# Four token tiles of the second layer, summed block by block beside w_out's conversion, in a one-core attention, cosine layer and expert-routing kernel

## The chip, the cores and the metric

The kernel runs on one core of a Trainium2 chip. The metric is the device time of one execution in microseconds; a lower number is better. The times below are medians of several runs; the rows come from one profiled execution, which has a time of its own.

## What is computed

Three stages follow each other; each takes the whole output of the one before.

```python
# 1. masked attention: 4 batches, 8 heads, 576 positions, head size 64
scores = scale * q @ k.T                  # heads 0-3: band of 32; heads 4-7: same position modulo 32
attn = softmax(where(masks, scores, -1e9)) @ v
x = attn.transpose(0, 2, 1, 3).reshape(2304, 512)
# 2. two layers with a cosine between them (d_ff = 2048)
h = x @ w_in
x = (h * cos(h)) @ w_out                  # 2304 x 512
# 3. routing to 8 experts with 288 places each, taken in order of all logits
logits = x @ w_gate
...
out[mask] = maximum(x[mask] @ w1[e], 0.0) @ w2[e]
```

Products are taken in float16 with a high and a low part, so that most matrix products are three matmuls: high by high, high by low, low by high. The input w_in and w_out are 8-byte floats and are converted on the chip.

## The kernel before, in words

A token tile is 128 of the 2304 tokens, so there are 18. A batch is 576 tokens. The **units** of the program are these; the short names are those used below.

- `att_pair(b, pr)` and `att_half(b, pr)` are a quarter of batch b's attention (two heads). They end in `x_parts`, which writes the layer's input x as two float16 parts into `xt`. VectorE takes row maxima, subtracts, sums and scales (tile `mxs` is in most of these).
- `load_w_in(f)` and `load_w_out(f)` fetch one of 16 blocks of a weight (512 KB) and convert it to two float16 parts. For w_out, VectorE, ScalarE and GpSimd share the work in `ar_t`; then a transposing DMA and eight small matmuls into PSUM bank `WP_BANK` = 7 multiply the block by w_gate (`wp`), so that later tiles can have their logits straight from layer one's output.
- `l1_unit(b, f)` is **layer one** for batch b and block f: two halves of 288 tokens, each 12 matmuls of 288 columns into one of PSUM banks 0 to 3; then a chain of ScalarE, VectorE and sometimes GpSimd gives h cos(h) as two float16 parts in `gt0` and `gt1` (tile `ar_g`). The bank is free when VectorE has read it the second time.
- `l2_tile(c)` is **layer two** for tile c: 48 matmuls of 512 columns over 16 blocks, three per block, into one bank; then ScalarE and VectorE write two parts into `ys`, which goes to DRAM. `early_logits(c)` transposes `ys` by DMA and takes the logits of tiles 0 to 4.
- `route` picks the experts (a long chain on VectorE with matmuls between), beside layer two of tiles 7 to 17. `experts` runs the eight experts.

The program first records tasks with what they read and write; `Plan.order` then sets the order on each engine. It keeps a clock of its own with an estimate for each task and takes, on each engine, the ready task with the highest priority: the length of the way to the end, plus a number by label from the table `BOOST`. The table `CHOICE` says for many small steps which engine does them. The order that comes out is fixed; on the chip, each engine runs its list from top to bottom and waits where it must. Until the first matmul of w_out's product the planner fills TensorE's planned gaps with **filler** matmuls of 128 columns that compute nothing (`p.filler`, line 609); the constant `fill_to` marks that first product, and after it there are none.

Before, layer one of batch 0 lay beside batch 1's attention; the conversion of w_out came after it, beside layer one of both batches; tiles 0 to 6 of layer two came after w_out, beside batch 2's attention:

```python
    for f in range(8):
        load_w_in(8 + f)
        l1_unit(0, 8 + f)
        l1_unit(1, f)
        if f % 2:
            load_w_out(f // 2)
```

The numbers of lines that the profile shows are those of helpers: 458 a matmul, 465 a transpose on TensorE, 482 and 485 ScalarE, 494 VectorE, 536 and 539 GpSimd, 543 a DMA, 547 a transposing DMA, 609 a filler.

Of the kernel before, what the change touches and what calls it, by code (L numbers as in the profile page):

```python
# [52 lines left out]
BOOST = {
    ('att', 0, 0, 0): 8538, ('att', 0, 0, 1): -17834, ('att', 0, 0, 2): 21893, ('att', 0, 0, 3): 254876, ('att', 0, 0, 4): -11936,
    ('att', 0, 1, 0): -88250, ('att', 0, 1, 1): 15713, ('att', 0, 1, 2): 6391904, ('att', 0, 1, 3): -16350,
    ('att', 0, 1, 4): 27537, ('att', 0, 2, 0): -15655, ('att', 0, 2, 1): -6151125, ('att', 0, 2, 2): 25706,
    ('att', 0, 2, 3): 18105, ('att', 0, 2, 4): -3603, ('att', 0, 3, 0): -102223, ('att', 0, 3, 1): 3933, ('att', 0, 3, 2): 4578,
    ('att', 0, 3, 3): 1293507, ('att', 0, 3, 4): 55587, ('att', 1, 0, 0): 385344, ('att', 1, 0, 1): -13827,
    ('att', 1, 0, 2): -3257, ('att', 1, 0, 3): 7190412552, ('att', 1, 0, 4): 30834, ('att', 1, 1, 0): 332375,
    ('att', 1, 1, 1): -28707, ('att', 1, 1, 2): 12945, ('att', 1, 1, 3): 293834, ('att', 1, 1, 4): -12205,  # L60
    ('att', 1, 2, 0): -14904, ('att', 1, 2, 1): -2120, ('att', 1, 2, 2): 19248, ('att', 1, 2, 3): 23623, ('att', 1, 2, 4): 9916,
    ('att', 1, 3, 0): -40947, ('att', 1, 3, 1): 410022, ('att', 1, 3, 2): 734082, ('att', 1, 3, 3): 205386,
    ('att', 1, 3, 4): -2577446, ('att', 2, 0, 0): 170034, ('att', 2, 0, 1): -130164, ('att', 2, 0, 2): 1120,
    ('att', 2, 0, 4): 13844, ('att', 2, 1, 0): 173621, ('att', 2, 1, 1): 176249, ('att', 2, 1, 2): -16793,
    ('att', 2, 1, 3): -27505, ('att', 2, 1, 4): -21043, ('att', 2, 2, 0): 227709, ('att', 2, 2, 1): 232256,
    ('att', 2, 2, 2): 21657, ('att', 2, 2, 3): 24684, ('att', 2, 2, 4): 12233196, ('att', 2, 3, 0): 245937,
    ('att', 2, 3, 1): -7701, ('att', 2, 3, 2): -3872, ('att', 2, 3, 3): 42822, ('att', 2, 3, 4): 4790463, ('att', 3, 0, 0): 20913,
    ('att', 3, 0, 1): -3804, ('att', 3, 0, 2): 27666, ('att', 3, 0, 3): -40439, ('att', 3, 0, 4): -70359, ('att', 3, 1, 0): -2201,
    ('att', 3, 1, 1): -10465, ('att', 3, 1, 2): -90149, ('att', 3, 1, 3): 936780, ('att', 3, 1, 4): -10007, ('att', 3, 2, 0): 2485,
    ('att', 3, 2, 1): -2493, ('att', 3, 2, 2): 16812, ('att', 3, 2, 3): -16129, ('att', 3, 2, 4): 18634, ('att', 3, 3, 0): 65330,  # L70
# [1629 lines left out]
```

## Time and profile before

| | |
|---|---|
| median of 3 runs | 774.19 us (773.64 to 775.09) |
| the profiled execution's own time | 779.23 us |
| its span in the trace | 777.4 us |
| TensorE busy | 716.3 us, 92% of the span |
| VectorE busy | 514.4 us, 66% |
| ScalarE busy | 424.6 us, 55% |
| GpSimd busy | 316.9 us, 41% |
| mean granted TensorE clock | 0.972 of full speed |

A share of the whole span is a mean over stages with different limits, so the rows below go by stretches. PE stands for TensorE, DVE for VectorE, ACT for ScalarE, POOL for GpSimd, SP for the queue that issues the DMAs. Times are in us from the span's start.

### The profile page before, as it was taken

The page shows a single profiled execution, that of the slowest core. Times are in us where ns is not written, and L with a number is a line of the kernel's source. Part 1 is how long each engine was busy: PE and PEld are TensorE (multiplying, and loading weights), DVE is VectorE, ACT ScalarE, POOL GpSimd, SP SyncE. Part 2 cuts the span into 40 slices and gives each one's busy share as a digit, 9 for nine tenths or more (in the row PEclk, how much of TensorE's full clock was granted, in tenths as well). Part 3 has the DMA queues.
Part 4 walks back from the last instruction along what each step waited for, and adds up shares of the span by engine and source line. Part 5 has one row for each costly group of instructions (what it writes and reads, how often), then busy time and mean ns, then how long its engine had stood idle before and what let it go on. Part 6 is the DMA issues. An engine that isn't in the chain of part 4 may idle for free. (4 is left out here: it accounts for less than half of the span.)

```text
span 777.4 us, 19249 instructions
## 1 busy us (share of the span) xinstructions
PE 716.3 (92%) x7714; PEld 515.1 (66%) x7714; DVE 514.4 (66%) x1392; ACT 424.6 (55%) x946; POOL 316.9 (41%) x344
## 2 busy tenths in 40 slices
PE   8999978999999999988999999997799989799986
PEld 7788756676455567666774555555687767577766
DVE  5787888989475777774568798878145435445550
ACT  3544967896444568986874243010146645555662
POOL 1538545486754025534431122011534446452531
PEclk9999989999999999999989999999799999899999
DMA  8944434566669644300023334001568879988771
GB/s 247 284 136 131 84 110 109 122 137 143 145 157 198 162 114 104 56 20 1 1 82 127 105 119 153 17 1 56 123 153 217 231 203 215 214 209 220 210 211 32
DMA packets 114265, 104.18 MB, mean 134 GB/s; under 512 B 79872, under 2 KB 89856, under 8 KB 114176
## 3 DMA queue, kind: packets, MB, share of 16 engines
q1 hardware_dynamic: 111104, 93.52, 47.8%
q0 software_dynamic: 3072, 9.44, 4.0%
q8 instruction: 60, 0.98, 0.5%
q14 instruction: 29, 0.24, 0.1%
HBM read 74.36 MB, written 9.70 MB: 108 GB/s over the span
## 5 line engine op out<-in xcount | busy, mean ns | idle before, releaser
L458 PEld LDWEIGHTS <-ar_l 128*128 128x128 f16 x2576 | 235.2, 100 | 98.9 <-issue 37.5
L458 PE MATMUL psum<-ar_w,ar_g 128*128 128x512 f16 (+2 forms) x1248 | 227.3, 319 | 2.8 <-DVE ar_w L494 1.8
L458 PE MATMUL psum<-ar_l 128*128 128x288 f16 (+2 forms) x1578 | 206.5, 286 | 20.8 <-DVE ar_l L494 17.8
L458 PEld LDWEIGHTS <-ar_g 128*128 128x128 f16 (+1 forms) x1944 | 151.4, 98 | 94.5 <-issue 7.0
L482 ACT ACTIVATE ar_l<-psum 128x288 int32<-128x288 f32 (+5 forms) x199 | 78.2, 424 | 73.3 <-PE psum L458 59.1
L494 DVE SCALAR_TENSOR_TENSOR ar_l<-ar_l,psum 128x288 f32<-128x288 int32 (+4 forms) x220 | 94.2, 449 | 36.1 <-ACT ar_l L482 35.1
L539 POOL TENSOR_TENSOR ar_l<-ar_l 128x288 f32<-128x288 f32 (+2 forms) x65 | 51.8, 800 | 157.1 <-DVE ar_l L494 82.0
L458 PEld LDWEIGHTS <-ar_t 128*128 128x128 f16 (+3 forms) x1900 | 73.0, 101 | 43.6 <-issue 11.8
L482 ACT ACTIVATE ar_g<-ar_l 128x512 f16<-128x512 f32 (+4 forms) x183 | 82.1, 474 | 35.3 <-DMA ar_l<-w 25.1
L539 POOL TENSOR_TENSOR ar_g<-ar_l,ar_g 128x288 f16<-128x288 f32 (+3 forms) x82 | 67.5, 830 | 57.4 <-ACT ar_g L482 56.7
L482 ACT ACTIVATE ar_l<-ar_l 128x512 f16<-128x512 f32 (+1 forms) x87 | 51.7, 623 | 53.5 <-DMA ar_l<-w 49.0
L482 ACT ACTIVATE ar_l<-ar_l,quarter 128x288 f32<-128x288 f32 (+1 forms) x124 | 64.6, 540 | 7.9 <-DVE ar_l L494 7.1
L458 PE MATMUL psum<-ar_g 128*128 128x288 f16 (+4 forms) x720 | 63.8, 264 | 5.1 <-ACT ar_g L482 2.5
L482 ACT ACTIVATE ar_t<-ar_t 128x512 uint32<-128x512 uint32 (+10 forms) x65 | 47.6, 747 | 37.5 <-DVE ar_t L494 8.7
L458 PE MATMUL psum<-ar_w,ar_t 128*128 128x512 f16 (+1 forms) x240 | 65.6, 336 | 0.0
L494 DVE SCALAR_TENSOR_TENSOR ar_l<-ar_l 128x512 f16<-128x512 f32 (+3 forms) x82 | 42.9, 546 | 31.8 <-ACT ar_l L482 29.3
L494 DVE SCALAR_TENSOR_TENSOR ar_t<-ar_t 128x512 uint32<-128x512 uint32 (+6 forms) x59 | 51.0, 867 | 14.6 <-ACT ar_t L482 14.6
L458 PE MATMUL psum<-ar_g,ar_l 128*128 128x96 f16 (+1 forms) x576 | 53.4, 255 | 7.5 <-DVE ar_w L494 4.4
L539 POOL TENSOR_TENSOR ar_t<-ar_t 128x512 uint32<-128x512 uint32 (+6 forms) x25 | 41.8, 1670 | 45.4 <-ACT ar_t L482 44.9
L458 PE MATMUL psum<-ar_w,ar_l 128*128 128x288 f16 x384 | 50.7, 295 | 3.7 <-DVE ar_w L494 3.7
L494 DVE SCALAR_TENSOR_TENSOR ar_g<-ar_l,ar_g 128x512 f16<-128x512 f32 x45 | 33.5, 768 | 29.7 <-ACT ar_g L482 28.9
L494 DVE SCALAR_TENSOR_TENSOR ar_w<-psum,ar_w 128x288 f16<-128x288 f32 x64 | 28.1, 451 | 27.1 <-ACT ar_w L482 26.5
(132 smaller groups left out, 829.4 us busy)
## 6 DMA issues: line engine op xcount, KB each, us to landing
...
```

The lines of the kernel that those rows point to most:

```text
L458: nc.tensor.matmul(o, l, x, start=start, stop=stop)
L482: p.add("act", ns, lambda: nc.scalar.activation(o, x, func, **kw), r, w, tab=tab)
L494: p.add("dve", 69.0 + 1.042 * n, lambda: getattr(nc.vector, name)(*args, **kw), r, w, ports=both)
L539: p.add("pool", 145.0 + (rate or (1.667 if y.dtype == F32 else 1.885)) * size(o), lambda: nc.gpsimd.tensor_tensor(o, x, y, op=op), r, w, p ...
```

## The change

Four tiles (0 to 3, `FIRST_TILES`) of layer two are recorded ahead of batch 1's layer one. All of w_in and of batch 0's layer one is recorded first, then w_out's 16 blocks with the rest of batch 1's attention between them, then the four tiles, then layer one of batch 1. Since the tiles 0 to 3 hold tokens of batch 0 alone, each needs only batch 0's layer one and those blocks of w_out that it has come to. Their outputs and transposed copies lie in that part of `gt1` that batch 1's layer one fills last (blocks 8 to 15), which is given a key of its own (`gB`), so that these writes wait until the four tiles are stored. The product of w_out and w_gate moves to columns 384 to 447 of bank 7 and the early logits to columns 480 to 495 of bank 4, with keys of their own (`wpb`, `lgp`) in place of the banks' keys. The tables `BOOST` and `CHOICE` are new nearly throughout: 373 of the 408 numbers of `BOOST` differ, 35 are gone and 17 new; of `CHOICE`, 24 entries differ, 84 are gone and 99 new.

```diff
-L2_GROUP, EARLY_TILES, EARLY_LOGITS, MORE_STAGE = 1, 7, 5, 8
+L2_GROUP, EARLY_TILES, EARLY_LOGITS, MORE_STAGE, FIRST_TILES = 1, 7, 5, 8, 4
...
-    ('att', 0, 0, 0): 8538, ('att', 0, 0, 1): -17834, ('att', 0, 0, 2): 21893, ('att', 0, 0, 3): 254876, ('att', 0, 0, 4): -11936,
...
-            mm(g, qk + kk_ + [("ident16",), ("mask16",)], pk(sbank[h]))
+            mm(g, qk + kk_ + [("ident16",), ("mask16",)], pk(sbank[h]) + ([("wpb",)] if sbank[h] == WP_BANK else []))
...
-        pw = bank[WP_BANK][:, :64].rearrange("p (f i e) -> p f i e", f=4, i=2)
+        pw = bank[WP_BANK][:, 384:448].rearrange("p (f i e) -> p f i e", f=4, i=2)
...
-        mm(g, [ck, ("wgh",)], pk(WP_BANK))
+        mm(g, [ck, ("wgh",)], [("wpb",)])
...
+    def gkey(key, f, i):
+
+        return (("gB" if key[0] == "gb" and f >= 8 else key[0]), *key[1:], f, i)
...
+        first = c < FIRST_TILES
...
+        yk = [("yt8", c)] if first else [("x", 1, pr, i, r) for pr in (2 * j, 2 * j + 1) for r in range(2)]
...
+        if first:
+            pl, bk = bank[4][:, 480:496], [("lgp",)]
+        else:
+            bi = take()
+            pl, bk = bank[bi][:, :16], pk(bi)
...
-    for f in range(8):
+    for f in range(16):
         load_w_in(f)
-        steps(att, 3 if f % 2 else 2)
         l1_unit(0, f)
-    steps(att, 2)
     p.reuse(["mask32", "stage1", "cv1"], ["woh", "wol"])
-    for f in range(8):
-        load_w_in(8 + f)
-        l1_unit(0, 8 + f)
+
+    yss[:] = [gt1[:, 1, 8 + 2 * c:10 + 2 * c].rearrange("p a b -> p (a b)") for c in range(FIRST_TILES)]
+    for f in range(16):
+        load_w_out(f)
+        steps(att, 1 + f % 2)
+    for c in range(FIRST_TILES):
+        yi, ys = l2_tile(c, hbank)
+        early_logits(c, ys, yi, hbank)
+    steps(att, 100)
+    p.reuse(["ys", "yt8"], ["gB"])
+    for f in range(16):
         l1_unit(1, f)
-        if f % 2:
-            load_w_out(f // 2)
-    for f in range(8):
-        load_w_out(4 + f)
-        l1_unit(1, 8 + f)
-    for f in range(12, 16):
-        load_w_out(f)
...
-    for c in range(early_tiles):
+    steps(att, 5 * FIRST_TILES)
+    for c in range(FIRST_TILES, early_tiles):
         yi, ys = l2_tile(c, hbank)
```

Three places show what this does to the lists of the engines. The first is the start of the DMA queue's list. In the rows `kl`, `q` are the inputs of batch 0's first attention quarter, `w_in` a block of 512 KB. Before:

```order
L543 DMA ar_w<-mask 128x304
L543 DMA ar_g<-kl 128x352
L543 DMA ar_g<-q 128x320
L543 DMA ar_g<-kl 128x256
L543 DMA ar_g<-q 128x256
```

And of the change:

```order
L570 DMA ar_t<-w_in 128x4x256 x2
L570 DMA ar_w<-w_in 128x4x256 x2
L570 DMA ar_w<-mask 128x304
L570 DMA ar_w<-w_in 128x4x256
L570 DMA wg<-w_gate 128x32
L570 DMA ar_g<-kl 128x352
L570 DMA ar_g<-q 128x320
L570 DMA ar_g<-kl 128x256
```

Five blocks of w_in now stand ahead of the first attention input. On TensorE, 711 fillers stand in the list of the change where 507 stood: 234 ahead of the first attention matmul (35 before), and 516 ahead of the first matmul of layer one (128 before). The other 6870 matmuls are the same in number.

The second place is TensorE's list right behind the product of w_out's block 6 with w_gate (`wgh`). A row `ar_l 128x288` is a matmul of layer one, `ar_w,ar_g 128x512` one of layer two. Before:

```order
L458 LDWEIGHTS ar_t
L458 MATMUL psum<-wgh,ar_t 128x8
L458 LDWEIGHTS ar_l
L458 MATMUL psum<-ar_l 128x288
L458 LDWEIGHTS ar_l
L458 MATMUL psum<-ar_l 128x288
```

And of the change:

```order
L485 LDWEIGHTS ar_t
L485 MATMUL psum<-wgh,ar_t 128x8
L485 LDWEIGHTS ar_g
L485 MATMUL psum<-ar_w,ar_g 128x512
L485 LDWEIGHTS ar_g
L485 MATMUL psum<-ar_w,ar_g 128x512
L485 LDWEIGHTS ar_l
L485 MATMUL psum<-ar_l 128x288
```

The first matmuls of tile 0 stand there, with nine blocks of w_out to come; between this block and the last one the list holds 126 matmuls of layer two, where 74 stood before.

The third place is VectorE's list in batch 2's attention (`mxs`), around its second block of scores. `ar_l<-ar_l,psum 128x288` is a step of a layer-one unit. Before:

```order
L494 TENSOR_REDUCE mxs<-psum 128x5
L494 TENSOR_REDUCE mxs<-psum 128x4
L494 TENSOR_TENSOR ar_t<-psum,mxs 128x480
L494 TENSOR_TENSOR ar_t<-psum,mxs 128x384
L494 TENSOR_REDUCE mxs<-ar_t 128x5
L494 TENSOR_SCALAR lgl_78<-psum 128x8
L494 SCALAR_TENSOR_TENSOR ar_t<-ar_t 128x1152
L494 SCALAR_TENSOR_TENSOR lg<-psum,lgl_78 128x8
L494 TENSOR_REDUCE mxs<-ar_t 128x4
```

And of the change:

```order
L521 SCALAR_TENSOR_TENSOR ar_l<-ar_l,psum 128x288
L521 TENSOR_REDUCE mxs<-psum 128x5
L521 TENSOR_REDUCE mxs<-psum 128x4
L521 TENSOR_TENSOR ar_t<-psum,mxs 128x480
L521 TENSOR_TENSOR ar_t<-psum,mxs 128x384
L521 TENSOR_SCALAR lgl_77<-psum 128x8
L521 SCALAR_TENSOR_TENSOR ar_l<-ar_l,psum 128x288
L521 SCALAR_TENSOR_TENSOR lg<-psum,lgl_77 128x8
L521 TENSOR_REDUCE mxs<-ar_t 128x5
L521 TENSOR_REDUCE mxs<-ar_t 128x4
```

Batch 2's attention now shares VectorE with layer one of batch 1; before it stood between evictions of layer-two tiles.

## Rows read from the trace of the kernel before

**Rows 1.** The page: its head, and what the DMAs moved in 40 slices.

```profile
span 777.4 us, 19249 instructions
...
GB/s 247 284 136 131 84 110 109 122 137 143 145 157 198 162 114 104 56 20 1 1 82 127 105 119 153 17 1 56 123 153 217 231 203 215 214 209 220 210 211 32
```

**Rows 2.** Busy time of each engine in seven stretches of the span.

```profile
core 0: us, PE busy (x) PEld busy (x) DVE busy (x) ACT busy (x) POOL busy (x), PEclk, DMA share, GB/s
0.00:90.70 90.70, 85.52 (x1339) 71.66 (x1340) 69.84 (x152) 47.70 (x113) 43.37 (x51) 1.00 0.66 186
90.70:178.00 87.30, 76.46 (x689) 58.35 (x687) 77.92 (x162) 70.49 (x186) 52.68 (x60) 0.96 0.49 115
178.00:272.00 94.00, 92.94 (x946) 51.34 (x945) 62.81 (x115) 46.02 (x89) 42.64 (x34) 1.00 0.72 161
272.00:346.00 74.00, 67.99 (x931) 51.45 (x928) 55.89 (x126) 62.73 (x132) 32.35 (x28) 1.00 0.35 77
346.00:398.00 52.00, 48.34 (x407) 37.86 (x406) 28.05 (x61) 39.93 (x105) 23.05 (x30) 1.00 0.05 16
398.00:546.00 148.00, 140.62 (x1436) 79.86 (x1434) 121.11 (x600) 40.31 (x72) 25.16 (x39) 0.96 0.24 81
546.00:777.40 231.40, 204.43 (x1980) 164.60 (x1980) 98.81 (x183) 117.41 (x253) 97.60 (x105) 0.94 0.76 188
```

**Rows 3.** PE's waits: in 90.7:178, in 272:346, and two in 346:398.

```profile
PE psum L458 <- DVE ar_l L494: 10.8, 12, 4.3
...
PE psum L458 <- DVE ar_l L494: 5.7, 8, 1.3
...
PE psum L458 <- ACT ar_l L482: 2.6, 3, 1.3
PE psum L458 <- DVE ar_l L494: 1.0, 2, 0.6
```

**Rows 4.** The filler's tile; then busy time of line 609 in two stretches.

```profile
L609 PE MATMUL psum<-quarter x507: 216/222/314, 0.9 to 90.6; 128*128 128x128 f16 x169
...
0.00:4.40 4.40, 3.51 (x34) 3.51 (x35) 1.00 0.53 149
38.50:41.40 2.90, 2.72 (x47) 2.73 (x48) 1.00 0.61 187
```

**Rows 5.** Groups by form: layer one 346.5:396, layer two 247.5:256, VectorE 132:207, 207:272.

```profile
L458 PE MATMUL psum<-ar_l 128*128 128x288 f16 x364 | 46.1, 286 | 3.7 <-ACT ar_l L482 2.6 <-DVE ar_l L494 1.0
...
L458 PE MATMUL psum<-ar_w,ar_g 128*128 128x512 f16 x34 | 7.5, 379 | 0.0
...
L494 DVE SCALAR_TENSOR_TENSOR ar_l<-ar_l,psum 128x288 f32<-128x288 int32 x35 | 15.3, 448 | 3.7 <-ACT ar_l L482 3.5
L494 DVE TENSOR_SCALAR ar_t<-ar_t 128x512 uint32<-128x512 uint32 x11 | 7.4, 673 | 1.9 <-PE psum L458 1.3 <-POOL ar_w L539 0.6
...
L494 DVE SCALAR_TENSOR_TENSOR ar_t<-psum,ar_t 128x512 f16<-128x512 f32 x5 | 3.4, 686 | 0.7 <-ACT ar_t L482 0.7
```

**Rows 6.** Busy time of each engine in two stretches, columns as in Rows 2.

```profile
132.00:207.00 75.00, 70.75 (x580) 49.34 (x579) 63.87 (x127) 56.56 (x152) 54.31 (x58) 1.00 0.57 128
...
207.00:272.00 65.00, 64.15 (x735) 34.34 (x734) 41.50 (x75) 28.87 (x44) 20.93 (x13) 1.00 0.78 175
```

**Rows 7.** The same of instructions on tile ar_t alone, in three stretches.

```profile
34.00:97.00 63.00, 17.88 (x374) 13.72 (x374) 26.09 (x42) 13.17 (x31) 20.75 (x18) 1.00 0.47 132
...
132.00:207.00 75.00, 4.16 (x96) 4.02 (x96) 26.85 (x35) 11.75 (x19) 27.53 (x22) 1.00 0.57 128
...
207.00:272.00 65.00, 12.07 (x405) 10.40 (x405) 29.83 (x40) 25.29 (x35) 20.93 (x13) 1.00 0.78 175
```

**Rows 8.** Instructions on tile mxs, 34:104: busy DVE, ACT, POOL, then clock.

```profile
34.00:104.00 70.00, 13.68 (x32) 2.30 (x9) 6.84 (x4) 1.00 0.45 127
```

**Rows 9.** Busy time in the stretch at the lower granted clock, columns as in Rows 2.

```profile
108.40:115.30 6.90, 4.48 (x19) 2.75 (x19) 6.54 (x15) 5.57 (x14) 4.65 (x5) 0.51 0.47 153
```

**Rows 10.** PE's longest wait in 546:777.4: us in total, times, longest.

```profile
PE psum L458 <- DVE ar_w L494: 10.6, 7, 3.9
```

More of the change, by code (lines that the diff above doesn't have):

```diff
@@ L50 @@
 S_BANKS, S2_BANKS, X_BANKS, T_BANKS, WP_BANK = (4, 4), (4, 7), (5, 6), (7,), 7
-L2_GROUP, EARLY_TILES, EARLY_LOGITS, MORE_STAGE = 1, 7, 5, 8
+L2_GROUP, EARLY_TILES, EARLY_LOGITS, MORE_STAGE, FIRST_TILES = 1, 7, 5, 8, 4
 BOOST = {
-    ('att', 0, 0, 0): 8538, ('att', 0, 0, 1): -17834, ('att', 0, 0, 2): 21893, ('att', 0, 0, 3): 254876, ('att', 0, 0, 4): -11936,
[L55 to L70, printed above, removed]
[72 rows of a table removed]
@@ new lines @@
+    ('att', 0, 0, 0): 64768, ('att', 0, 0, 1): 180, ('att', 0, 0, 2): 123215, ('att', 0, 0, 3): 372907, ('att', 0, 0, 4): -61505,
+    ('att', 0, 1, 0): -30903, ('att', 0, 1, 1): 3914, ('att', 0, 1, 3): -29192, ('att', 0, 1, 4): 1103431, ('att', 0, 2, 0): 40980,
+    ('att', 0, 2, 1): 1914, ('att', 0, 2, 2): 1937, ('att', 0, 2, 3): -196979022, ('att', 0, 3, 0): 9004, ('att', 0, 3, 1): -1977,
+    ('att', 0, 3, 2): 1888421, ('att', 0, 3, 3): 40429, ('att', 0, 3, 4): 64601, ('att', 1, 0, 0): 532, ('att', 1, 0, 1): 21303,
@@ new lines @@
+    ('att', 1, 1, 0): 554072, ('att', 1, 1, 1): -486, ('att', 1, 1, 3): 644979, ('att', 1, 1, 4): -1647, ('att', 1, 2, 0): 215,
+    ('att', 1, 2, 1): -288897, ('att', 1, 2, 2): 61280369, ('att', 1, 2, 3): 211675996, ('att', 1, 2, 4): -44884,
+    ('att', 1, 3, 0): 66239546, ('att', 1, 3, 1): 1912602, ('att', 1, 3, 2): -16835267,
+    ('att', 1, 3, 3): 2292248208926377539181100400640, ('att', 1, 3, 4): 32451, ('att', 2, 0, 0): 40171891,
+    ('att', 2, 0, 1): 60380, ('att', 2, 0, 2): -396115, ('att', 2, 0, 3): 11289, ('att', 2, 0, 4): 4621, ('att', 2, 1, 0): 653038,
@@ new lines @@
+    ('att', 2, 1, 1): 390, ('att', 2, 1, 2): -16698, ('att', 2, 1, 3): 207087, ('att', 2, 1, 4): -25471, ('att', 2, 2, 0): 138573,
+    ('att', 2, 2, 1): 141862, ('att', 2, 2, 2): 11323, ('att', 2, 2, 3): 4966, ('att', 2, 2, 4): 281999176557,
+    ('att', 2, 3, 0): -1126, ('att', 2, 3, 1): -364522544032689451672166440056582256332202049536, ('att', 2, 3, 3): -6305,
+    ('att', 2, 3, 4): -43370778662819572853743805874402027687116800,
+    ('att', 3, 0, 0): 101041401800544194786443176735291514269204480, ('att', 3, 0, 2): -43294, ('att', 3, 0, 3): -73,
@@ L143 @@
+    ('att', 3, 0, 4): 9222, ('att', 3, 1, 2): -10643, ('att', 3, 1, 3): 4688129, ('att', 3, 1, 4): -5518516531986,
+    ('att', 3, 2, 0): -115, ('att', 3, 2, 1): -314, ('att', 3, 2, 2): 16713, ('att', 3, 2, 3): -8722721700,
+    ('att', 3, 2, 4): -17524, ('att', 3, 3, 0): 668, ('att', 3, 3, 1): 487558, ('att', 3, 3, 2): -108061,
[93 rows of a table added]
 }
 CHOICE = {
-    ('cvi', 0): 'pool', ('cvi', 2): 'pool', ('cvi', 9): 'pool2', ('cvi', 10): 'pool', ('cvi', 14): 'pool', ('cvo', 5): 'pool2',
+    ('cvi', 0): 'psum', ('cvi', 2): 'pool', ('cvi', 9): 'pool2', ('cvi', 10): 'pool', ('cvi', 14): 'pool', ('cvo', 5): 'pool2',
@@ L197 @@
-    ('pts', 0, 0, 2): 'dve', ('pts', 0, 1, 2): 'dve', ('pts', 0, 2, 0): 'dve', ('pts', 0, 2, 1): 'dve', ('pts', 0, 2, 2): 'dve',
-    ('pts', 0, 3, 0): 'dve', ('pts', 0, 3, 1): 'dve', ('pts', 0, 3, 2): 'dve', ('pts', 1, 0, 0): 'dve', ('pts', 1, 0, 1): 'dve',
-    ('pts', 1, 0, 2): 'dve', ('pts', 1, 1, 0): 'dve', ('pts', 1, 2, 2): 'dve', ('pts', 1, 3, 1): 'dve', ('u', 0, 0): 'halves',
[14 rows of a table removed]
-    ('ylo', 8): 'dve', ('ylo', 9): 'dve', ('ylo', 11): 'dve', ('ylo', 12): 'dve', ('ylo', 13): 'dve', ('ylo', 15): 'dve',
@@ L215 @@
-    ('yt', 0, 1): 'act', ('yt', 2, 0): 'dve',
+    ('ewa', 0, 'w1', 0, 512): 'pool2', ('ewa', 0, 'w1', 1, 0): 'pool', ('ewa', 0, 'w1', 1, 512): 'pool',
+    ('ewa', 0, 'w1', 2, 0): 'pool', ('ewa', 0, 'w1', 3, 512): 'pool', ('ewa', 0, 'w2', 3, 0): 'pool',
+    ('ewa', 0, 'w2', 7, 0): 'pool', ('ewa', 1, 'w1', 1, 0): 'pool2', ('ewa', 1, 'w1', 1, 512): 'pool',
+    ('ewa', 1, 'w1', 2, 0): 'pool', ('ewa', 1, 'w1', 3, 512): 'pool', ('ewa', 1, 'w2', 5, 0): 'pool',
+    ('ewa', 2, 'w1', 0, 0): 'pool', ('ewa', 2, 'w1', 1, 512): 'pool', ('ewa', 2, 'w1', 3, 0): 'pool',
[4 rows of a table added]
@@ new lines @@
+    ('ewa', 4, 'w2', 5, 0): 'pool', ('ewa', 4, 'w2', 6, 0): 'pool2', ('ewa', 5, 'w1', 1, 0): 'pool',
+    ('ewa', 5, 'w1', 2, 0): 'pool2', ('ewa', 5, 'w1', 3, 0): 'pool2', ('ewa', 5, 'w2', 0, 0): 'pool',
+    ('ewa', 5, 'w2', 7, 0): 'pool2', ('ewa', 6, 'w1', 0, 0): 'pool', ('ewa', 6, 'w1', 0, 512): 'pool2',
+    ('ewa', 6, 'w1', 1, 0): 'pool', ('ewa', 6, 'w1', 2, 512): 'pool', ('ewa', 6, 'w2', 1, 0): 'pool2',
+    ('ewa', 6, 'w2', 2, 0): 'pool', ('ewa', 6, 'w2', 3, 0): 'pool2', ('ewa', 6, 'w2', 4, 0): 'pool',
@@ new lines @@
+    ('ewa', 7, 'w1', 1, 0): 'pool', ('ewa', 7, 'w1', 1, 512): 'pool2', ('ewa', 7, 'w1', 2, 512): 'pool',
+    ('ewa', 7, 'w2', 6, 0): 'pool', ('exp', 0, 0): 'bias', ('exp', 0, 1): 'bias', ('exp', 1, 1): 'bias', ('g', 0, 4, 1): 'pool',
[24 rows of a table added]
+    ('hv', 2, 0): 'pool', ('hv', 3, 1): 'pool', ('hv', 3, 3): 'pool', ('mul', 0, 1): 'dve', ('mul', 0, 2): 'dve',
+    ('mul', 2, 1): 'pool', ('mul', 2, 3): 'pool', ('mul', 3, 0): 'pool', ('mul', 3, 2): 'pool', ('og', 0, 0, 0): 'act',
[12 rows of a table added]
+    ('oh', 6, 3, 1): 'dve', ('plo', 2, 1): 'pool', ('plo', 2, 2): 'pool', ('plo', 2, 3): 'pool', ('plo', 3, 0): 'pool',
@@ new lines @@
+    ('plo', 3, 3): 'pool', ('pts', 0, 3, 1): 'dve', ('pts', 1, 0, 0): 'dve', ('pts', 1, 0, 1): 'dve', ('pts', 1, 0, 2): 'dve',
+    ('pts', 1, 1, 0): 'dve', ('pts', 1, 2, 2): 'dve', ('u', 0, 0): 'halves', ('u', 0, 1): 'halves', ('u', 0, 2): 'halves',
[14 rows of a table added]
+    ('xl', 0, 3, 0): 'pool', ('xl', 1, 2, 0): 'pool', ('xl', 1, 3, 0): 'pool', ('ylo', 8): 'dve', ('ylo', 9): 'dve',
+    ('ylo', 11): 'dve', ('ylo', 12): 'dve', ('ylo', 13): 'dve', ('ylo', 15): 'dve', ('yt', 0, 0): 'dve', ('yt', 0, 1): 'act',
+    ('yt', 2, 0): 'dve', ('yt', 2, 1): 'act',
@@ L477, in act_fixed @@
     def act_fixed(r):
-        return 51.0 if any(k[0] == "ps" for k in r) else 92.0
+        return 51.0 if any(k[0] in ("ps", "wpb", "lgp") for k in r) else 92.0
     def act(o, x, func, r, w, tab=None, **kw):
@@ L491, in call @@
             def call(n, r, w, *args, **kw):
-                on_psum = any(k[0] == "ps" for k in list(r) + list(w))
+                on_psum = any(k[0] in ("ps", "wpb", "lgp") for k in list(r) + list(w))
                 both = not on_psum and name in ("tensor_tensor", "scalar_tensor_tensor", "tensor_scalar", "tensor_copy")
@@ L972, in load_w_out_ @@
             lk = [("lgl", li)]
-            act(ll, pw[:, :, 1], AF.Copy, pk(WP_BANK), lk, scale=1.0 / WOUT_SCALE)
-            dve.scalar_tensor_tensor(32, pk(WP_BANK) + lk, lk, ll, pw[:, :, 0], 1.0 / WOUT_SCALE, ll, op0=ALU.mult, op1=ALU.add)
+            act(ll, pw[:, :, 1], AF.Copy, [("wpb",)], lk, scale=1.0 / WOUT_SCALE)
+            dve.scalar_tensor_tensor(32, [("wpb",)] + lk, lk, ll, pw[:, :, 0], 1.0 / WOUT_SCALE, ll, op0=ALU.mult, op1=ALU.add)
             act(wp[:, fs, :NE], ll, AF.Copy, lk, k0)
@@ L1040, in l1_unit_ @@
             for lo, hi, gt, at, keys in pieces:
-                k0, k1 = ([(*k, f, i) for k in keys] for i in range(2))
+                k0, k1 = ([gkey(k, f, i) for k in keys] for i in range(2))
                 gh, gl = (gt[:, i, f, at:at + hi - lo] for i in range(2))
@@ L1065, in g_segments @@
                     segs.append([gt, at + lo, hi - lo, keys])
-        return [(gt, o, n, lambda f, keys=keys: [(*k, f, i) for k in keys for i in range(2)]) for gt, o, n, keys in segs]
+        return [(gt, o, n, lambda f, keys=keys: [gkey(k, f, i) for k in keys for i in range(2)]) for gt, o, n, keys in segs]
     def logits(c0, take, after=()):
@@ L1096, in early_logits @@
         i, j = divmod(c % 4, 2)
-        yt = xt[1][:, i, 2 * j:2 * j + 2, :].rearrange("p k t -> p (k t)")[:, :1024].rearrange("p (i k t) -> p i k t", i=2, t=128)
-        yk = [("x", 1, pr, i, r) for pr in (2 * j, 2 * j + 1) for r in range(2)]
+        first = c < FIRST_TILES
+        yt = gt1[:, 0, 8 + 2 * c:10 + 2 * c].rearrange("p a b -> p (a b)").rearrange("p (i k t) -> p i k t", i=2, t=128) if first else xt[1][:, i, 2 * j:2 * j + 2, :].rearrange("p k t -> p (k t)")[:, :1024].rearrange("p (i k t) -> p i k t", i=2, t=128)
+        yk = [("yt8", c)] if first else [("x", 1, pr, i, r) for pr in (2 * j, 2 * j + 1) for r in range(2)]
         dma_t(yt.rearrange("p i k t -> p (i k) t"), ys, [("ys", yi, j, h) for j in range(2) for h in range(2)], yk)
-        bi = take()
-        pl = bank[bi][:, :16]
+        if first:
[3 more added lines that the diff above has]
+            pl, bk = bank[bi][:, :16], pk(bi)
         g = []
@@ L1105, in early_logits @@
             g.append((pl[:, :NE], yt[:, 1, k], wgh[:, 0, k, :], False, k == 3))
-        mm(g, yk + [("wgh",)], pk(bi))
+        mm(g, yk + [("wgh",)], bk)
         ll, lk = rot("lgl", lgl)[::-1]
         scale = 1.0 / (WOUT_SCALE * Y_SCALE)
-        dve.tensor_scalar(8, pk(bi), [("lgl", lk)], ll[:, 0], pl[:, NE:], scale, None, op0=ALU.mult)
-        dve.scalar_tensor_tensor(8, pk(bi) + [("lgl", lk)], [("lg", c // 3 * 3)], lg[:, c, :], pl[:, :NE], scale, ll[:, 0],
+        dve.tensor_scalar(8, bk, [("lgl", lk)], ll[:, 0], pl[:, NE:], scale, None, op0=ALU.mult)
+        dve.scalar_tensor_tensor(8, bk + [("lgl", lk)], [("lg", c // 3 * 3)], lg[:, c, :], pl[:, :NE], scale, ll[:, 0],
                                  op0=ALU.mult, op1=ALU.add)
@@ L1519 @@
     p.label = None
-    p.reuse(["pqt", "pkt", "pvt", "psb", "ppts", "pxf"], ["ga", "gb", "gc"])
+    p.reuse(["pqt", "pkt", "pvt", "psb", "ppts", "pxf"], ["ga", "gb", "gc", "ys", "yt8"])
     ar_g.at = 0
@@ L1610 @@
         p.series = None
-    p.reuse(["gb"], ["w11", "w21"])
+    p.reuse(["gb", "gB"], ["w11", "w21"])
     p.reuse(["ga", "gc"], ["yt", "yg", "og", "ot"])
```

14 lines of the change are left out of this document (removed), and 268 rows, old and new, of tables (BOOST, CHOICE).

## The prediction

> **What bounds the kernel now.** I read the busy time by stretch first [rows 2]. TensorE is the busiest engine in every stretch but one, so the question for each stretch is how long TensorE stood still and for whom. Up to 90.7 it shows 85.5 busy of 90.7, but the fillers' tile [rows 4] says that 507 of the matmuls there compute nothing; the last one starts at 90.6. In this part VectorE (69.8 busy) and the arriving weights set the pace and TensorE is padded. From 90.7 to the end of layer one at 398, TensorE is busy for 76.5 + 92.9 + 68.0 + 48.3 = 285.7 of 307.3, so 21.6 are lost. The chain of waits names the loser's partner [rows 3]: 10.8 for VectorE in 90.7:178, where w_out is converted beside layer one and VectorE is busy for 77.9 of 87.3; 5.7 for VectorE in 272:346, where batch 3's attention lies beside layer one of batch 2; 2.6 for ScalarE and 1.0 for VectorE in 346:398. In 178:272, where layer two gives TensorE long work that asks little of VectorE, only 1.1 are lost. From 398 on (routing beside layer two, then the experts) the change edits no code but tables.
>
> So the kernel is bound by TensorE where layer two is at hand and by VectorE where conversions, attention and layer one meet. The change moves layer two to the first kind of trouble, and leaves the second kind, batch 2's attention, without part of it.
>
> **The change, term by term.**
>
> *More fillers.* 711 − 507 = 204 fillers are added, and TensorE runs its list in order, so each is paid. In mid-program 47 fillers take 2.72 [rows 4], 0.058 each; 204 × 0.058 = **+11.8**. They don't come on top of real work done in the same time: they stand where real work stood. At the last filler the list of before has 520 real matmuls behind it and that of the change 399, of which 36 missing ones are layer one's (46.1 / 364 = 0.127 each [rows 5], 4.6) and 85 batch 1's attention (17.9 / 374 = 0.048 per record and two records for many [rows 7], so 4 to 8). That makes 9 to 12, about what the fillers take; so the last filler ends at about the same time as before, near 91, with some 12 of work still to do. Is VectorE further by then, so that this is paid back? By its list, the work ahead of that point is w_in nearly whole instead of two thirds, but less of the attention and of layer one: 132 instructions against 147. I take no gain.
>
> *The start.* The first scores now stand behind five blocks of w_in and the mask, some 3.1 MB. At the first slice's 247 GB/s [rows 1] that is 12.6. The 234 fillers ahead of them take 35 at 3.51 / 34 = 0.103 [rows 4] and 199 at 0.058, in all 15.1, from 0.9 on: until 16.0. The load is hidden by 3.4; should it take longer than that, the rest would be paid in full, since every later attention step follows it. Taken as nothing.
>
> *Stretch I, from the last filler to w_out's last block.* TensorE's list: 288 matmuls of layer one (36.5), 126 of layer two at 7.5 / 34 = 0.22 [rows 5] (27.8), and 241 small ones at 0.043 to 0.048 [rows 7] (11): 75. VectorE's: twelve units of layer one, fourteen blocks of w_out, half of batch 1's attention. Prices from 132:207, where nothing else runs on it: 63.9 busy [rows 6], of which 26.9 on `ar_t` [rows 7] and about 2.5 for the product with w_gate are w_out's, and 34.5 layer one's. The 35 first steps are 17.5 units, the 11 conversions 11 blocks [rows 5]; so 2.0 per unit and 2.7 per block. 24 + 37 + half of 13.7 [rows 8] = 68, or 0.90 of TensorE's.
>
> *Stretch II, from there to the end of layer one of batch 1.* TensorE: 384 of layer one (48.8), 98 of layer two (21.6), 378 small ones at 12.07 / 405 = 0.030 [rows 7] (11): 81.5. VectorE: 16 units (32), four evictions at 0.69 [rows 5] (2.8), and batch 2's attention with its loads: 41.5 busy in 207:272 [rows 6] less 3.4 for five evictions and 1.6 for logits = 36.5. Together 71, or 0.87. Before, this attention had layer two beside it.
>
> *Stretch III, to the end of layer one of batch 2*, holds what 272:346 held, with 112 matmuls of layer two (24.7) in place of 27: TensorE 68.0 + 85 × 0.22 = 87, VectorE about 60 (55.9 and the end of batch 2's attention), 0.69. *Stretch IV* is batch 3's layer one as before.
>
> *What is lost in them.* The trace gives loss against load: at a ratio of VectorE to TensorE of 0.68 (178:272) 1% of TensorE's time, at 0.82 (272:346) 9%, at 1.02 (90.7:178) 14% [rows 2]. Between these, 0.90 gives 11% of 75 = 8.3, and 0.87 gives 10% of 81.5 = 8.2. Layer two in the list can run while VectorE catches up, so I take off its share of TensorE's work (27.8 of 75, 21.6 of 81.5): 5.2 and 6.0. For III I take 2.5 (between 1.3, by the ratio, and the 6.0 of 272:346), for IV the 3.7 of now. In all **17.4** where 21.6 are lost now. Bounds: below, nothing in I and II, 6.2 in all; above, 14% in both, 6.0 and 3.7, in all 32.
>
> *The clock.* In 108.4:115.3 the granted clock is 0.51, the lower of the two levels, 1.2 GHz; the longest wait of rows 3, 4.3, lies just ahead of it. TensorE was busy for 4.48 of these 6.9 [rows 9]; at 2.4 GHz it would need half, so up to 2.2 come back if the wait goes and the clock stays up. I take **−1.1**. The Trainium skill ("TensorE: Matmul & The Clock Gate", section "Terms") puts the penalty at the throttled time times what is missing of the clock, here 3.4; the row gives less, since a third of that stretch had no matmul to slow. With the page's figure taken whole, the sum below would be 4.2 instead of 6.5.
>
> *At nothing:* the keys `wpb` and `lgp` only take waits away, and PE's waits show none for that product; tiles 0 to 3 are stored and transposed once as before, only sooner. The new wait is that of `gB`: batch 1's layer one may not write block 8 until the fourth tile's logits are read. Behind it would stand ScalarE and VectorE, and TensorE for their banks. But 98 matmuls stand on TensorE between those logits and block 8's first half, 60 of them layer one's (7.6); a store and a transpose have that long. Were the cover gone, it would cost what is missing of a few microseconds once. From 398 on: the same matmuls, other tables. TensorE loses 27 of the last 231.4 there [rows 2], 10.6 of them in its longest wait [rows 10]; I take 0 and bounds of ±3, about a tenth of it.
>
> *The sum.* 11.8 − 21.6 + 17.4 − 1.1 = **+6.5**. On the span 777.4 this makes 783.9, and with the 1.8 that the profiled execution has around its span, 785.7. That execution, 779.23, stands 5.0 above the median of the runs, 774.19; so I forecast a median of **780.7**.
>
> **The rivals.** *Faster.* Layer two's blocks, three matmuls each, cover all of VectorE's lag in I and II, and the losses fall to 6.2; with the clock kept, 11.8 − 21.6 + 6.2 − 2.2 = −5.8, **768.4**. It decides at losses of 9.4: below, the change wins by more than 0.2% (1.55 of 774.19, about what a measurement tells from no change). For it speaks 178:272, where 1% is lost beside layer two; against it, that VectorE had 0.68 there and has 0.87 to 0.90 now, and that layer two is a third and a quarter of the list instead of two thirds.
>
> *No change.* Losses of 9.4 to 12.5, a little under what the ratio and the cover give: **774**.
>
> *Much slower.* The small share of layer two covers nothing, since a bank must be free for its tile too, and both stretches lose 14%: 11.8 − 21.6 + 32 = +22, **796**. Against it: VectorE's ratio is lower than where 14% was lost.
>
> That the change does not do what it says is excluded: the lists show layer two between w_out's blocks.
>
> **How the numbers follow.** My forecast, slower by 1.6 to 14: 0.54. Much slower, beyond that: 0.10. Faster: 0.23. No change: 0.13. So slower 0.64. The forecast's own range is 776 to 788. For 8 in 10, I leave one tenth at each end: **769 to 790**, from nearly all of the faster case to past the forecast's end.
>
> **What would show it.** After: the last filler near 91 and 711 of them, not 507, the last busy time of line 609; PE's wait for VectorE in the w_out stretch 4 to 7 instead of 10.8; a new wait for VectorE of 4 to 8 where `mxs` and `ar_l` steps alternate, at 170 to 260; layer one of batch 3 ending near 404 to 405 instead of 398; from there to the end 379 as now. The step most likely to fail is the loss in I and II: if PE waits less than 3 in either, the forecast is too high. If the last filler comes well before 88, the first term is wrong, and if it comes after 94, the start is.

## The result and the profile after

The change makes the kernel slower: 785.75 us (median of 4 runs, 784.71 to 786.54) against 774.50 of the kernel before (4 runs, 773.64 to 775.09), a ratio of 1.0145, 95% interval 1.0128 to 1.0163. That is +11.25, where +6.5 was forecast (780.7; 785.75 lies in the range 769 to 790). A second set of runs gave 783.99 against 774.20, 1.0114 (1.0081 to 1.0147), +9.8. So the sign and the range held, and the size was 3 to 5 too small. The profiled execution of the change has an own time of 784.71 and a span of 782.6.

Busy time of each engine in seven stretches of the change, cut at the last filler, w_out's last block, the end of layer one of batches 1, 2 and 3, the end of routing and the end of TensorE's work (columns as in [rows 2], which cut the kernel before at other times; ends of parts, here and below, are those of the last matmul of the part in TensorE's list):

```profile
0.00:89.30 89.30, 85.46 (x1357) 74.67 (x1358) 72.30 (x139) 47.00 (x108) 37.99 (x43) 1.00 0.71 216
89.30:171.70 82.40, 77.61 (x748) 50.63 (x746) 66.39 (x133) 59.04 (x136) 48.98 (x46) 0.98 0.52 129
171.70:259.90 88.20, 81.67 (x865) 56.81 (x863) 67.05 (x151) 72.26 (x153) 29.29 (x33) 1.00 0.50 126
259.90:350.10 90.20, 85.30 (x1056) 59.70 (x1054) 60.00 (x130) 67.11 (x142) 35.43 (x33) 1.00 0.30 76
350.10:401.30 51.20, 49.99 (x492) 39.91 (x490) 30.32 (x67) 41.69 (x110) 23.55 (x31) 1.00 0.02 6
401.30:551.20 149.90, 138.75 (x1436) 79.37 (x1434) 121.46 (x592) 41.68 (x75) 30.69 (x45) 0.97 0.24 84
551.20:775.60 224.40, 203.28 (x1982) 162.65 (x1981) 96.65 (x166) 118.97 (x257) 115.15 (x126) 0.95 0.77 193
```

Length minus TensorE's busy time, the first two numbers behind each stretch, is what TensorE lost: 3.8 up to the last filler, then 4.8, 6.5, 4.9 and 1.2 up to the end of layer one, together 17.4. The forecast for stretches I to IV was 17.4. Layer one ends at 401.3 (397.9 before). Up to there the change loses 3.4. Unless the shown profile of before is itself too long up to there (the second profile below answers this), the rest of the 11 lies behind it, where only the tables differ.

The filler's tile in the change, which answers to [rows 4]:

```profile
L636 PE MATMUL psum<-quarter x711: 216/222/315, 0.9 to 89.2; 128*128 128x128 f16 x178
```

PE's waits in 89.3:171.7, in 171.7:259.9 and in 259.9:350.1, which answer to [rows 3] (what is waited for: us in total, times, longest):

```profile
PE psum L485 <- DVE ar_l L521: 1.4, 4, 0.7
PE psum L485 <- ACT ar_l L509: 1.3, 1, 1.3
PE psum L485 <- DMA ar_t<-ar_w: 1.1, 2, 0.8
...
PE psum L485 <- DVE ar_l L521: 4.7, 6, 1.5
...
PE psum L485 <- DVE ar_l L521: 2.8, 4, 1.1
```

Beside w_out's conversion the wait for VectorE fell from 10.8 to 1.4; a new one of 4.7 stands beside batch 2's attention. PE's waits from the end of routing on, which answer to [rows 10]:

```profile
PE psum L485 <- ACT ar_g L509: 10.3, 5, 4.3
PE psum L485 <- DVE ar_w L521: 6.3, 7, 2.0
PE psum L485 <- DMA ar_g<-y_dram,idx: 3.8, 1, 3.8
```

The wait for ScalarE on `ar_g` is new in this size: in the experts ScalarE writes there the high parts of every second expert's weights.

### The profile page after: what moved, and what is told of

It is laid out like the page before. It is cut to its first block, busy times and chain, and to the rows that moved or that the text cites. A ratio compares the mean times of both kernels' runs of the same rounds, so it can differ in the third digit from the quotient of the medians.

```text
span 782.6 us, 19708 instructions
## 1 busy us (share of the span) xinstructions
PE 722.2 (92%) x7918; PEld 523.7 (67%) x7918; DVE 514.2 (66%) x1374; ACT 448.3 (57%) x979; POOL 322.0 (41%) x357
## 4 chain that ended last, share of the span: by engine, by line
PE 48%; DVE 14%; ACT 14%; DMA 12%; POOL 5%; issue 4%; SPq 2%; POOLq 0%; DVEq 0%; ACTq 0%
PE psum L485 43%; DMA ar_l<-w 6%; ACT ar_l L509 6%; DVE ar_l L521 6%; PE psum L636 4%; DVE ar_t L521 3%; ACT ar_t L509 3%; DVE mxs L521 2%; ACT ar_g L509 2%; DVE ar_g L521 2%; ACT L509 2%; POOL ar_l L566 2%; SPq L574 1%; DMA ar_g<-ar_g 1%; DMA ar_t<-ks 1%
## 5 line engine op out<-in xcount | busy, mean ns | idle before, releaser
L485 PEld LDWEIGHTS <-ar_l 128*128 128x128 f16 x2544 | 230.1, 98 | 82.4 <-issue 23.0
L485 PE MATMUL psum<-ar_w,ar_g 128*128 128x512 f16 (+2 forms) x1248 | 223.7, 318 | 5.7 <-DVE ar_w L521 3.5
L509 ACT ACTIVATE ar_l<-psum 128x288 int32<-128x288 f32 (+6 forms) x198 | 78.1, 420 | 73.4 <-PE psum L485 59.9
L566 POOL TENSOR_TENSOR ar_l<-ar_l 128x288 f32<-128x288 f32 (+2 forms) x78 | 66.3, 852 | 127.5 <-DVE ar_l L521 69.3
L485 PEld LDWEIGHTS <-ar_t 128*128 128x128 f16 (+3 forms) x1900 | 73.5, 101 | 45.9 <-issue 11.8
L485 PE MATMUL psum<-ar_g 128*128 128x288 f16 (+4 forms) x720 | 67.0, 268 | 11.7 <-ACT ar_g L509 10.3
L566 POOL TENSOR_TENSOR ar_t<-ar_t 128x512 uint32<-128x512 uint32 (+8 forms) x25 | 40.1, 1606 | 45.4 <-ACT ar_t L509 32.5
L521 DVE SCALAR_TENSOR_TENSOR ar_l<-ar_l 128x512 f16<-128x512 f32 (+4 forms) x68 | 38.0, 575 | 30.1 <-ACT ar_l L509 28.7
L509 ACT ACTIVATE ar_t<-ar_t 128x512 uint32<-128x512 uint32 (+11 forms) x65 | 47.1, 744 | 17.2 <-DMA ar_t<-kl 6.5
L485 PE MATMUL psum<-ar_w,ar_t 128*128 128x512 f16 (+1 forms) x240 | 56.9, 336 | 0.0
L636 PE MATMUL psum<-quarter 128*128 128x128 f16 x711 | 48.0, 227 | 2.4 <-DVE ar_t L521 1.5
```

The source lines that it names most:

```text
L485: nc.tensor.matmul(o, l, x, start=start, stop=stop)
L509: p.add("act", ns, lambda: nc.scalar.activation(o, x, func, **kw), r, w, tab=tab)
L521: p.add("dve", 69.0 + 1.042 * n, lambda: getattr(nc.vector, name)(*args, **kw), r, w, ports=both)
L566: p.add("pool", 145.0 + (rate or (1.667 if y.dtype == F32 else 1.885)) * size(o), lambda: nc.gpsimd.tensor_tensor(o, x, y, op=op), r, w, p ...
L636: p.filler = lambda: nc.tensor.matmul(bank[7][:, 384:], some.to_broadcast([128, 128]), some.to_broadcast([128, 128]), start=True, stop=True)
```

## The experiments

One table first. The second column is its start, the next two are ends, "experts" is from the end of routing to TensorE's end, all from the kernel's one profiled execution, whose own time stands behind. The median is of all runs of that kernel, the ratio goes against runs of the kernel before on the same chip (medians 772.93, 774.20 and 775.64 in the three sets).

| kernel | first attention matmul | layer one of batch 3 | routing | experts | own time | median | ratio (95%) |
|---|---|---|---|---|---|---|---|
| before | 4.5 | 397.9 | 545.7 | 225.0 | 779.23 | 774.19 | |
| b_again | 4.3 | 397.5 | 546.3 | 217.5 | 772.34 | | |
| b_more_fill | 16.0 | 405.5 | 553.0 | 216.7 | 779.16 | 779.16 | 1.0083 (1.0050 to 1.0116) |
| b_tail_of_a | 4.4 | 397.5 | 553.0 | 226.1 | 787.63 | 785.71 | 1.0143 (1.0116 to 1.0169) |
| b_exp_of_a | 4.1 | 396.6 | 548.0 | 223.1 | 780.01 | 782.69 | 1.0097 (1.0061 to 1.0133) |
| after | 16.6 | 401.3 | 551.2 | 224.4 | 784.71 | 785.75 | 1.0145 (1.0128 to 1.0163) |
| a_again | 15.8 | 399.0 | 549.7 | 225.3 | 783.99 | 783.99 | 1.0114 (1.0081 to 1.0147) |
| a_less_fill | 12.8 | 397.6 | 547.0 | 223.8 | 779.75 | 784.15 | 1.0161 (1.0109 to 1.0212) |
| a_no_late_fill | 15.9 | 398.5 | 548.5 | 226.0 | 783.32 | 784.25 | 1.0155 (1.0101 to 1.0210) |
| a_att_first | 4.2 | 413.7 | 563.3 | 227.4 | 799.55 | 798.94 | 1.0309 (1.0282 to 1.0336) |
| a_tail_of_b | 16.4 | 401.1 | 562.1 | 217.6 | 788.84 | 784.18 | 1.0124 (1.0098 to 1.0150) |
| a_exp_of_b | 16.9 | 402.3 | 552.7 | 220.0 | 781.88 | 777.88 | 1.0010 (0.9981 to 1.0040) |
| a_conv_of_b | 17.1 | 401.4 | 551.7 | 224.8 | 785.28 | 784.66 | 1.0113 (1.0079 to 1.0147) |
| a_exp_of_b_less_fill | 12.9 | 399.5 | 548.9 | 223.0 | 780.80 | 778.61 | 1.0034 (1.0008 to 1.0060) |

**A second profile of before.** No edit.

> The kernel before, unchanged, for a second profile. The profiled execution of before was 5.0 longer than the median of its runs, so its rows overstate some stretch. My theory (the change's loss arises before routing, in layer one and what lies ahead of it): the end of layer one of batch 3 at 393 to 395 instead of 398 and the same 370 from the last logits to the end. Rival (the new order of routing and experts costs it): the end of layer one at 398 as before, and about 366 from the last logits to the end, against 371.8 in the change. Own time 774 by both.

The two profiles of before agree within 0.6 up to the end of routing and differ by 7.5 in the experts: the rows shown of before overstate that stretch, and no other. Busy time from the end of routing on, in the second profile (b_again):

```profile
546.30:763.80 217.50, 201.02 (x1982) 162.67 (x1981) 98.13 (x183) 117.15 (x252) 97.73 (x104) 0.96 0.79 199
```

And PE's waits there:

```profile
PE psum L458 <- DVE ar_w L494: 9.4, 7, 2.5
PE psum L458 <- DMA ar_g<-y_dram,idx: 3.8, 1, 3.8
PE psum L458 <- ACT ar_g L482: 3.1, 3, 1.8
```

Beside these the change has GpSimd busy for 115.15 instead of 97.73, and the wait on `ar_g` is 10.3 instead of 3.1. So the rival gained: the end of layer one is not 393 to 395 in this kernel, as my theory wanted, but 397.5.

**Fillers.** Three kernels: the change without its first 204 fillers, the change without the 477 behind the first attention matmul, and the kernel before with 199 more at its head.

```diff
-    for emit in p.order():
+    emits, dropped = p.order(), 0
+    for emit in emits:
+        if emit is p.filler and dropped < 204:
+            dropped += 1
+            continue
         emit()
```

> The change, in the same order, without the first 204 of its 711 fillers (507 are left, as many as before). The output is unchanged. My prediction charged these fillers with 11.8. If they hold real work back, the first attention matmul comes 10 sooner than 16.9 and the time falls by 8 to 12. If they stand in time that TensorE would wait in anyway, for the inputs of the attention and then for VectorE, the time stays within 1.5, and PE's waits ahead of the last filler rise from 3.7 to about 15.

> The change, in the same order, with the 234 fillers ahead of the first attention matmul alone; the other 477 are left out. If fillers hold real work back, the time falls by up to 27 (477 at 0.058). If they only fill waits, the last w_out block ends within 1.5 of where it did, and what changes is the granted clock: it drops to the lower level in parts of 17 to 90, and the time rises by 1 to 6.

> The kernel before with 199 more fillers at the head of TensorE's list, so that 234 stand ahead of the first attention matmul, as in the change, and nothing else is moved. It starts the first scores some 11 later. If the start of attention sets the pace of the first part, the time rises by 8 to 11; if the slack of the first part (507 fillers) takes it up, by 0 to 3.

Neither removal makes the change measurably faster: 1.0161 and 1.0155 stand beside the 1.0145 and 1.0114 of the change itself. With four runs each this excludes the 8 to 12 that would come back if each filler were paid, but not a gain of 2 or 3. PE's waits in 0:89 without the 204:

```profile
PE psum L485 <- DVE mask L521: 8.6, 1, 8.6
PE psum L636 <- DVE ar_t L521: 1.5, 2, 0.9
PE psum L636 <- POOL quarter L628: 0.9, 1, 0.9
PE psum L485 <- DVE ar_t L521: 0.8, 1, 0.8
```

The fillers' time came back as a wait of 8.6 for the mask and the inputs behind it. The first attention matmul starts at 12.8 instead of 16.6 (the prediction had 12.6 for the transfers), and what that gains is still there in this one execution at the end of routing (547.0 against 551.2 and 549.7), but not in the medians.

Busy time in 16:89.2 and 89.2:171.2 without the 477:

```profile
16.00:89.20 73.20, 54.01 (x660) 39.04 (x658) 62.55 (x123) 43.14 (x102) 32.67 (x31) 0.77 0.65 193
89.20:171.20 82.00, 75.19 (x735) 48.80 (x734) 65.93 (x131) 57.73 (x134) 47.81 (x46) 1.00 0.60 132
```

The granted clock is 0.77 there instead of 1.00, and w_out's last block still ends at 171.2 (171.7 and 171.0 with all fillers). By the Trainium skill ("TensorE: Matmul & The Clock Gate", section "Terms") the clock alone would cost 0.23 of 73.2, an estimate of 16.8. None of it is seen: even at the lower clock TensorE is busy for only 54.0 of the 73.2. So fillers are neither a cost nor a gain in this stretch.

In the kernel before, attention 11.7 later (16.0 instead of 4.3) makes the end of layer one 8.0 later, the end of routing 6.7, and the kernel 6.4 slower (1.0083), between the two expectations. There the start does set the pace, for somewhat more than half of the delay.

**The start in the change.** An order of my own: the attention inputs first, w_in's first conversions about 17 later, 313 fillers left out.

```diff
-    for emit in p.order():
-        emit()
+    for i in FROZEN:
+        for _ in range(max(1, -i)):
+            (p.filler if i < 0 else p.tasks[i][2])()
```

`FROZEN` is the whole order of issue, written out as task numbers; a negative number is so many fillers. The kernels below use it too, so their line numbers are higher.

> The change, with batch 0's attention started as early as in the kernel before: its inputs and the mask stand first in the list of the DMA queue, the first conversions of w_in stand some 17 later against them on every engine and meet the old order again by w_in's end, and 313 of the 711 fillers, which covered the later start, are left out. If the late start of attention (16.6 instead of 4.3) sets the pace of the first part, the end of layer one of batch 3 comes 5 to 10 sooner than 401.3, and the time is 776 to 781. If VectorE's work in all sets it, or the delayed w_in takes the place of the late attention, the end of layer one stays at 397 to 401 and the time at 782 to 786.

It came out at 798.94, outside both. The first attention matmul is at 4.2, but batch 0's attention still ends at 56.1 (56.3 in the change). VectorE's waits in 0:56:

```profile
DVE wgh L725 <- ACT wgh L713: 9.0, 1, 9.0
DVE mask L725 <- DMA ar_w<-mask: 2.9, 1, 2.9
```

With the inputs first, w_gate lands late, and the instruction that makes its low part had kept its early place on VectorE: the attention's steps there stood 9.0 behind it. Layer one of batch 0 then ends 13 later than in the change (160.4 against 147.4), which this wait doesn't explain; the later conversions of w_in may, but that isn't shown. The kernel tells of my order and not of the start; what an early start would be worth in the change stays open.

**The experts.** Two hybrids first, in which the whole weight conversion and the eight experts take the engines and the order of the other kernel, also those conversions (experts 0 and 1) that lie beside routing. 106 entries of `CHOICE` differ (three of them here, one to a line).

```diff
 CHOICE = {
-    ('ewa', 2, 'w1', 1, 512): 'pool',
+    ('ewa', 2, 'w2', 7, 0): 'pool',
-    ('ewa', 3, 'w1', 0, 512): 'pool2',
...
-    for emit in p.order():
-        emit()
+    for i in FROZEN:
...
```

> The change, unchanged, for a second profile and more times. By the theory that the experts' stretch of the change is itself slower, it takes 223 to 226 again from the end of routing to TensorE's end (224.4 in the first profile; 217.5 in the second one of before), and the median is 784 to 787. By the rival, that the stretch only varies from one execution to the next, as between the two profiles of before (225.0 and 217.5), a stretch of 217 to 219 must turn up here or in the other kernels that share this order.

> The change, with its eight experts alone as in the kernel before: the choice of engine for the conversions and copies of that stretch, and the order of its instructions among themselves and against those of routing; the rest stands in the order of the change. If the experts' tables cost about 7 of the 11.25, the time falls to 777 to 780, GpSimd is busy for 97 there instead of 115, and PE's wait for ScalarE on ar_g there falls from 10.3 to about 3.5. If the loss lies ahead of the experts, 784 to 787.

> The mirror: the kernel before, with its eight experts alone as in the change. If the experts' tables cost about 7, 779 to 782 (773 to 774.5 plus 7) and 223 to 226 from the end of routing on. If the loss lies ahead of the experts, 773 to 775.

The experts' stretch goes with the tables and not with the kernel around it: 217.6 in the change with the experts of before, 226.1 in the mirror. But the change gained nothing in all (784.18): routing, from the end of layer one on, took 161.0 instead of 149.9, with the other kernel's conversions of experts 0 and 1 between its steps. The mirror's 785.71 has 155.5 there instead of 148. So I left what lies beside routing alone, and exchanged only what follows it: the weights of experts 2 to 7, gathers, both layers, stores (98 entries, edited as above). One more kernel keeps the change's order and takes only the engines of the conversions from before (34 of these entries).

> The change, up to the end of routing in its own order and with its own engines (the weights of experts 0 and 1, which are converted beside routing, among them); from there on the experts as in the kernel before: the weights of experts 2 to 7, gathers, both layers, stores, with their engines and their order. If the tables of the experts cost 7 to 8, routing takes 140 to 141 as in the change, the experts 217 to 218 instead of 224 to 225, and the time is 776 to 778. If what was saved there comes back in routing, as in the first hybrid, 783 to 785.

> The mirror: the kernel before up to the end of routing, and from there on the experts as in the change. If their tables cost 7 to 8, routing takes 139, the experts 224 to 226, and the time is 781 to 783; if not, 773 to 775.

> The change, in its own order throughout; only the engines that make the low parts of the weights of experts 2 to 7 are chosen as in the kernel before: in 20 half blocks VectorE in place of GpSimd, in 10 GpSimd in place of VectorE, in 4 another step on GpSimd. If GpSimd's greater share holds the staging buffers longer, so that late weights make TensorE wait (4.3 ahead of expert 7's first layer), the experts take 217 to 221 and the time is 776 to 781. If the order of the instructions costs it, the experts stay at 223 to 227 and the time at 783 to 787.

With the experts of before, the change takes 777.88, 6 to 8 less than its 783.99 and 785.75 in the other sets and 6.8 less than a_conv_of_b in the same set, and is no longer to be told from the kernel before (1.0010, 0.9981 to 1.0040). With the experts of the change, the kernel before takes 782.69, by the ratio +7.5 (4.7 to 10.3). So most of the loss is there. With only the engines exchanged nothing comes back (784.66). Routing took 150.4 in a_exp_of_b, as in the change (149.9), so this time nothing was lost there; the 140 to 141 and the 139 of the expectations fit no profile as the table counts. PE's wait for ScalarE on `ar_g` from the end of routing on, in a_again:

```profile
PE psum L485 <- ACT ar_g L509: 8.6, 6, 4.1
```

The same in a_exp_of_b, with the experts of before:

```profile
PE psum L1227 <- ACT ar_g L1251: 2.7, 3, 1.1
```

In b_exp_of_a, with the experts of the change:

```profile
PE psum L1251 <- ACT ar_g L1275: 7.2, 4, 4.0
```

And in a_conv_of_b, with the order of the change and the engines of before:

```profile
PE psum L1228 <- ACT ar_g L1252: 9.1, 4, 3.8
```

The wait goes with the order, whatever the engines and the kernel ahead. What is late: each weight block comes through one of two staging buffers, and a buffer is loaded again when its block has been converted. The last 32 of these loads, those of experts 4 to 7, by their tile in b_again (durations of the issue, then first and last start):

```profile
L543 SPq DMA_DIRECT2D ar_l<-w x32: 327/378/961, 625.1 to 746.0; - x32
```

The same loads in the change:

```profile
L570 SPq DMA_DIRECT2D ar_l<-w x32: 327/368/1431, 630.0 to 758.1; - x32
```

In a_exp_of_b:

```profile
L1312 SPq DMA_DIRECT2D ar_l<-w x32: 327/373/1233, 633.5 to 755.2; - x32
```

And in a_conv_of_b:

```profile
L1313 SPq DMA_DIRECT2D ar_l<-w x32: 328/370/677, 630.7 to 759.1; - x32
```

From first to last issue that is 120.9 and 121.7 in the order of before, 128.1 and 128.4 in that of the change. Over all profiles: 120.9 to 123.7 in six, 125.9 to 130.8 in eight; no value of one kind lies among the other. The lengths of the experts themselves do overlap (216.7 to 225.0 and 223.1 to 227.4), since the start of the 32 loads varies too: in the first profile of before they begin 83.5 after the end of routing, in the second 78.8, which is most of the 7.5 between the two. In all fourteen profiles TensorE's work ends 17.3 to 18.2 after the last of these issues, so the experts are over when this stream is. In the list of the DMA queue, the change issues from expert 4 on the second block of each pair ahead of the first, in all 16 pairs; the order of before keeps them in the order of use. The block that ends the 4.3 (the third of expert 7's w1) is loaded some 192 after the end of routing in the change and 181 in b_again. Shown is that the order of the experts' instructions costs the 6 to 8. That the swap itself does, and not another place in the same order, was not tried apart.

**Both edits together.**

> The change with the experts as in the kernel before, and without the first 204 of its 711 fillers. If the two costs found so far are apart from each other (7 to 8 in the experts, 2 to 4 for a start that the fillers hold up), the first attention matmul comes at 12.8, layer one of batch 3 ends at 397 to 398 as in the kernel before, and the time is 773 to 775, not to be told from it. If fillers cost nothing, 776 to 778 as without this edit. A time under 772.5 would beat both kernels.

It came out at 778.61, 1.0034 (1.0008 to 1.0060), with the first attention matmul at 12.9 and layer one's end at 399.5: the fillers' removal adds nothing to the exchange of the experts, and no version was found that beats the kernel before.

## Why the prediction was right, and where it was not

*Fillers, +11.8.* Their count, their price and the end of the last one (89.3; forecast near 91) were right, and so was the sentence that this stretch ends at about the same time with more work left. But "each is paid" is wrong: without 204 or 477 of them the time is the same within what the runs tell. What they cover is the wait for inputs and for VectorE; the term measures that wait, and holding it for a price of the fillers would have promised a gain from removing them.

*The start, 0.* The transfers take until 12.8 (forecast 12.6) and the fillers until 16.9 (16.0), as said. That a later start is free was said only against these fillers; b_more_fill shows that in the kernel before a start 11.7 later costs 6.4. How much of that the change pays is open.

*The losses in I to IV, 17.4.* 4.8, 6.5, 4.9 and 1.2 against 5.2, 6.0, 2.5 and 3.7: the sum is exact by luck, since the misses in III and IV cancel and I is right in size but not in its cause. The wait for VectorE beside w_out is 1.4, less than the 4 to 7 named; the rest of the 4.8 are small waits, 1.3 for ScalarE and 1.1 for a transposing DMA the longest of them. In II the reading of ratio against loss carried: the new wait is 4.7, in its range of 4 to 8. The prediction's own sign (less than 3 of waiting in I or II: the forecast is too high) was met in I, and the forecast for the end of layer one was indeed too high; the whole was too low for another reason, below.

*The clock, −1.1.* The stretch at the lower clock did not go: 89.3:171.7 has a mean of 0.98 of the full clock, where 90.7:178 had 0.96 [rows 2]. The second profile of before has 0.98 over 90:178 too, so the term is within what varies between executions of one kernel.

*The sum to the end of layer one, +6.5.* 399.0 to 402.3 in the five profiles of the change's own order up to there, 396.6 to 397.9 in four of before: means of 401.0 and 397.4, +3.6. In the two shown profiles the last filler comes 1.4 sooner, the losses behind it are 4.2 less, as forecast, and TensorE's busy time there grows by about 9 (294.6 against 285.7) where 11.8 − 1.1 = 10.7 were forecast.

*From 398 on, 0 ± 3.* This is the step that failed. Routing is +1.0 (150.3 on the mean of four against 149.3 of three, without the two first hybrids). The experts are +5.1 by the means of all profiles (225.1 of eight in the order of the change, 220.0 of six in that of before, 216.7 to 225.0), and +6 to +8 by the exchanges in the times of whole runs. "The same matmuls, other tables" was true, and the new order there costs at least as much as all the edited stages. The shown profile hid it: from the end of layer one to the end of the span it has 379.5, the change 381.3, and the second profile of before 373.1.

The total of +9.8 to +11.25 so is 5 to 8 for the order in the experts and −1.5 to +5 for all ahead of it: +4.6 by the profiles (3.6 and 1.0), −0.2% to +0.4% by the times of a_exp_of_b. The runs do not part the two closer. My forecast had the second part at +6.5 and the first at nothing. So the right sign is luck in part: with the experts left as they were, the edited stages alone can't be told from no change, and what made the kernel clearly slower was a term that the forecast held at nothing. The faster rival needed losses under 9.4 and the one of no change under 12.5; there were 17.4, and the experts come on top. The much slower one needed 14% in both stretches; I and II lost 6% and 8%. Layer one and attention did meet on VectorE, at about the forecast price (6.5 lost in II, 6.0 forecast).
